# Local attention with a gated feed-forward layer on one core: the last scores of batch 0 placed ahead of its first value product, shifted values copied by GpSimd, and the first transposes of batch 1 moved to another PSUM pair

## The chip, the core and the metric

The kernel runs on one core of a Trainium2 chip. The metric is the device time of one execution in microseconds. In the text TensorE (PE in the profile, with its weight loads as PEld) does the matrix products and transposes, VectorE (DVE) and ScalarE (ACT) the elementwise work, GpSimd (POOL) and SP issue transfers; GpSimd also does a little elementwise work. L12 is line 12 of the kernel as the profile numbers it.

## The reference

Eight batches of eight heads attend over 576 tokens, with a window of 32 to either side and eight global tokens that see all and are seen by all. The result goes through a gated layer with 512 inputs and 1536 hidden columns.

```python
scores = scale * np.matmul(q, k.transpose(0, 1, 3, 2))
mask = np.abs(pos[:, None] - pos[None, :]) <= window
mask = mask | is_global[:, None] | is_global[None, :]
scores = np.where(mask, scores, -1000000000.0)
attn = softmax(scores)                       # over the keys
attn_out = np.matmul(attn, v)                # (8, 8, 576, 64)
x = attn_out.transpose(0, 2, 1, 3).reshape(4608, 512)
g = x @ w_gate
out = (g * sigmoid(g) * (x @ w_val)) @ w_out
```

## The kernel before

The attention of a batch is cut into steps, each a function that issues its instructions on all engines. In the order of the data they are:

- **step_T** (step_T0 for batch 0) transposes keys and queries of one pair of heads with TensorE (L355, L375) and copies them from PSUM into kT and qT. From batch 3 on a transposing DMA does this instead.
- **step_GT, step_SG, step_S2** handle the global tokens. GpSimd multiplies their gathered rows with a mask (kqm, L247), TensorE transposes them (L393), and products with all queries (SG) and all keys (S2) follow, each with an exponential and a mask product (pg at L416, p at L439).
- **step_P2T** transposes the masked S2 into p2t: by TensorE (L452) up to batch 3, by a transposing DMA from SP (L448) from batch 4 on. **step_AV2** multiplies p2t with the values (L462), and VectorE turns the sums into gvt (L469, L474, L477), which every value product of the batch reads.
- **step_S u**, u from 0 to 4, computes local scores: 64 queries against 128 keys a tile (L493), exponential on ScalarE (pe, L501), mask product on VectorE (pt, L507).
- **step_AV tp**, tp from 0 to 3, is the value product of 128 queries: a part from the global tokens (L546) and one from the window (L555), then the normalisation (den L522, L527 and xa L528). **step_AV8** does the last 64 queries.
- **step_X** transposes the result into xT, the input of the layer: by TensorE and a ScalarE copy (L604, L610) for batches 0 and 1, by a DMA later.

A value product takes its even 64-query tile from va, the values as loaded (128 tokens a block), and its odd one from **vb**, the same values shifted by 64 tokens. Since the shift crosses partitions, vb is made by a copy of each half of va into the other half of the partitions. Batch 0 makes it in vb0: VectorE copies the tiles 0 and 1 (L639, L640), two SP transfers the tiles 2 and 3 (L641, L642).

PSUM is held in three pools: "sc" (the score pair) and "m" with one pair of banks each, and "f" with four single banks. A step that allocates a buffer of a pool waits until the readers of the one that it replaces are done. Scores and some transposes lie in "sc", most of the other attention steps in "m", the layer's products in "f". For batch 0 several steps borrow "f", and the third gate of the first chunk (pgv) borrows "m".

The order of work is written out by hand, and each engine runs its instructions in the order in which they are issued. Batch 0 comes first, as one list of steps in which mask products and normalisations (the keys "p*", "xa*") are placed one by one, and warm(n), n products of constants into an unused "f" bank, stands between some of them. Behind it come the loads of batch 1 (loads_b, issued by GpSimd), and then the gates of the first 512 rows, column part by column part. From there on the layer's units (twelve gates, four outputs for each 512 rows) form a row of 144 slots, and the steps of batches 1 to 7 are dropped into the slots behind them. A batch b from 3 on has ten groups of steps that are spread over 16 slots from 16(b-1)+1 on.

A gate is eight products of 512 columns on TensorE (L711; L729 for the first two, done in parts), a tanh on ScalarE (th, L742) and two products on VectorE (gv, L744; h, L748); an output (L772) is twelve products and a ScalarE copy.

Of the kernel before, what the change touches and what calls it, by code (L numbers as in the profile page):

```python
# [26 lines left out]
def kernel(  # L27
# [11 lines left out]
    nc = tc.nc  # L39
# [32 lines left out]
    psc = ctx.enter_context(tc.tile_pool(name="psc", bufs=1, space=bass.MemoryType.PSUM))  # L72
    pm = ctx.enter_context(tc.tile_pool(name="pm", bufs=1, space=bass.MemoryType.PSUM))
# [50 lines left out]
    def load_vb(b):  # L124
        va = va_bufs[b % 2]
        vb = bp.tile([P, 4, H, W], BF16, tag="vb", name="vb")
        if b == 0:
            return vb
        nc.sync.dma_start(out=vb[0:64], in_=va[64:128, 0:4])
        nc.sync.dma_start(out=vb[64:128], in_=va[0:64, 1:5])  # L130
        return vb
# [39 lines left out]
    def clear(i):  # L171
# [10 lines left out]
        out=oh16.rearrange("p h a r -> p (h a r)"),  # L182
        in_=ident.rearrange("p (a g) -> p a g", g=NG), axis=AX.X, op=ALU.add,
# [3 lines left out]
        out=p8, in_=ident.rearrange("p (a g) -> p g a", g=NG), axis=AX.X, op=ALU.add  # L187
# [9 lines left out]
        out=tmp8h, in0=dmask.rearrange("p h r -> p (h r)"), in1=i8_f, op=ALU.mult  # L197
# [4 lines left out]
        out=gidx_f, in_=gidx_i64.bitcast(I32).rearrange("p (a b) -> p a b", b=2)[:, :, 0]  # L202
# [8 lines left out]
        out=hrow, in0=hrow, scalar1=float(S), scalar2=gcol, op0=ALU.mult, op1=ALU.add  # L211
# [4 lines left out]
        out=mka, in_=oh16.rearrange("p h a r -> p a r h"), axis=AX.X, op=ALU.add  # L216
# [6 lines left out]
        out=thr, in0=asel, scalar1=R2 + 0.25, scalar2=-0.25, op0=ALU.mult, op1=ALU.add  # L223
# [3 lines left out]
        out=sgn, in0=asel, scalar1=2.0, scalar2=-1.0, op0=ALU.mult, op1=ALU.add  # L227
# [3 lines left out]
        out=thi, in0=asel[:, 0:1], scalar1=1e6, scalar2=0.5, op0=ALU.mult, op1=ALU.add  # L231
# [13 lines left out]
    def gather_mask(kg, qg, kqm, eng=None):  # L245
        for a, src in ((0, kg), (1, qg)):
            (eng or nc.gpsimd).tensor_tensor(  # L247
                out=kqm[:, a], in0=bc(src, [[0, 2], [1, D]]),
                in1=bc(mka[:, a, :], [[1, 2], [0, D]]), op=ALU.mult,
            )  # L250
        return kqm
# [7 lines left out]
    def load_wgv(i):  # L259
# [13 lines left out]
        out=band, in_=band, compare_op=ALU.is_ge, fill=0.0,  # L273
# [3 lines left out]
        out=band, in_=band, compare_op=ALU.is_ge, fill=0.0,  # L277
# [60 lines left out]
    def attention(b):  # L338
        kT = kT_bufs[b % 2]
        va = va_bufs[b % 2]  # L340
        st = {}
# [21 lines left out]
        def step_T(hp):  # L363
            if hp == 0:
                qTs[b] = bp.tile([P, HP, S], BF16, tag="qT", name="qT")
            pool, tag = (pm, "m") if (hp in (0, 2) if b == 1 else hp == 3) else (psc, "sc")
            pair = pool.tile([P, 2, 1024], BF16, tag=tag, name="ps_t")
            pss = []
            for n, name in enumerate(("k", "q")):
                ps = pair[:, n, 0:S].rearrange("p (j i) -> p j i", j=LJ)  # L370
                pss.append(ps)
                src = loaded[b][name]
                for j in range(LJ):
                    for par in range(2):
                        nc.tensor.transpose(  # L375
                            out=ps[64 * par : 64 * par + 64, j, :],
                            in_=src[:, 2 * hp + par, D * j : D * (j + 1)],
                            identity=ident[0:LP, 0:LP],
                        )
            nc.scalar.copy(  # L380
                out=kT[:, hp, WIN : WIN + S].rearrange("p (i j) -> p i j", j=LJ),
                in_=pss[0].rearrange("p j i -> p i j"),
            )
            (nc.scalar.copy if hp % 2 else nc.vector.tensor_copy)(
                out=qTs[b][:, hp, :].rearrange("p (i j) -> p i j", j=LJ),
                in_=pss[1].rearrange("p j i -> p i j"),
            )
# [249 lines left out]
        def vb0(t):  # L637
            st["vb"] = load_vb(0)
            nc.vector.tensor_copy(out=st["vb"][0:64, 0:2], in_=va[64:128, 0:2])  # L639
            nc.vector.tensor_copy(out=st["vb"][64:128, 0:2], in_=va[0:64, 1:3])  # L640
            nc.sync.dma_start(out=st["vb"][0:64, 2:4], in_=va[64:128, 2:4])  # L641
            nc.sync.dma_start(out=st["vb"][64:128, 2:4], in_=va[0:64, 3:5])  # L642

        L = lambda f, *a: (lambda: f(*a))
        if b == 0:
            act, dve = nc.scalar.copy, nc.vector.tensor_copy

            M = lambda *key: (lambda: st[key if len(key) > 1 else key[0]]())
            def kqm0():
                kqms[0] = gather_mask(*g0, eng=nc.vector)  # L650

            return [
                L(squares), L(tables_a),
                L(step_T0, "k", 0, act), L(step_T0, "k", 1, act), L(tables_b), L(clear, 1),
                L(step_T0, "q", 0, act), L(step_T0, "q", 1, dve),
                L(step_T0, "k", 2, act), L(step_T0, "k", 3, act), kqm0, L(step_GT),
                L(step_S, 0), L(step_S2), M("p2*"), L(step_T0, "q", 2, dve),
                L(step_T0, "q", 3, act), L(step_P2T), L(step_SG), L(step_S, 1), M("p*", 0),
                L(vb0, 0), M("pg*"), L(step_AV2), M("p*", 1),
                L(step_S, 2), L(step_S, 3), L(warm, 2), L(step_AV, 0), M("p*", 2), M("xa*", 0),  # L660
                L(step_AV, 1), L(warm, 1), M("p*", 3), M("xa*", 1), L(step_X, 0),
                L(step_AV, 2), L(warm, 1), M("xa*", 2), L(step_X, 1), L(step_AV, 3), M("xa*", 3),
            ], [L(step_X, 2)], [L(step_X, 3)], [L(step_S, 4), M("p*", 4)], [L(step_AV8)], [L(step_X8)]
# [12 lines left out]
        if b < XQ:  # L676
            return [
                [L(step_T, 0)], [L(step_T, 1)],
                *([[L(step_T, 2)], [L(step_GT), L(step_T, 3), vb]] if b == 1 else
                  [[L(step_GT), L(step_T, 2)], [L(step_T, 3), vb]]),  # L680
            ] + mid + end
# [2 lines left out]
            [L(step_S2), L(step_SG)],  # L684
            [L(step_S, 0), L(step_P2T)],
            [],
            [L(step_S, 1)],
            [L(step_S, 2), L(step_AV2)],
            [L(step_S, 3), L(step_AV, 0), L(step_X, 0)],
            [L(step_AV, 1), L(step_X, 1)],  # L690
            [L(step_S, 4), L(step_AV, 2), L(step_X, 2)],
# [91 lines left out]


    head, xa2, xa3, s4, av8, x8 = attention(0)
    for f in head:
        f()
# [32 lines left out]
    for b, o in ((1, 2), (2, 15)):  # L820
        for i, g in enumerate(attention(b)):
            gaps[o + i] = gaps.get(o + i, []) + g
    for b in range(XQ, B):
        steps = attention(b)
        o = 16 * (b - 1)
        for i, g in enumerate(steps):
            slot = o + 1 + (16 * i) // len(steps)
            gaps[slot] = gaps.get(slot, []) + g
        if b > XQ:
            tr_at[b] = o - 16 + 5  # L830
        if b > 4:
            cast_at[b] = o - 32 + 8
        v_at[b] = o - 16 + 2
        g_at[b] = o - 16 + 6
        m_at[b] = o - 16 + 13
# [43 lines left out]
```

The softmax here doesn't subtract the row's maximum and nothing guards it: scores larger than these inputs give would overflow.

## Time and profile before

| | |
|---|---|
| median of six runs | 371.2 us (368.19 to 373.56) |
| the profiled execution | 370.38 us |
| its span | 368.7 us |
| mean granted clock of TensorE | 0.995 |
| busy: PE, DVE, ACT, POOL | 351.3, 235.4, 152.8, 97.5 us |
| matrix products of the layer's gates (L711) and outputs (L772) | 217.5 and 94.5 us |

The span runs from the first to the last instruction of one execution, and all times of the trace count from its start. The profiled execution's own time is 1.7 us longer than the span and 0.8 us under the median. A busy share is not the same as being the limit: the layer's products and the steps between them are what TensorE works through, and the other engines matter where TensorE waits for them. In the lines of the trace the first number is the start, the second the duration, both in us, and a bracket at the end gives how long the engine stood idle ahead of the row and what released it.

### The profile page before, as it was taken

How to read it: one execution, taken by the hardware profiler on the slowest of the kernel's cores; microseconds unless marked ns; L12 is line 12 of the kernel's file. 1: busy time of each engine (PE TensorE's matmuls, PEld its weight loads, DVE VectorE, ACT ScalarE, POOL GpSimd, SP SyncE). 2: the span in 40 equal slices, each digit the busy share in tenths (PEclk: the TensorE clock that was granted, in tenths of full speed). 3: DMA queues.
4: the chain of work that ended last, by engine and by line, in shares of the span. 5: the costliest groups of instructions: out<-in, count | busy, mean ns of one | idle time of the engine just before them, and what ended most of it. 6: DMA issues, size and time to landing. Idle time of an engine off the chain costs nothing.

```text
span 368.7 us, 7993 instructions
## 1 busy us (share of the span) xinstructions
PE 351.3 (95%) x3290; PEld 175.8 (48%) x3290; DVE 235.4 (64%) x469; ACT 152.8 (41%) x237; POOL 97.5 (26%) x114
## 2 busy tenths in 40 slices
PE   3786999999999999999999999999999999999996
PEld 2564545554544444444544445444544454444444
DVE  6665678268962885488548863887388728724750
ACT  5633574357422652255325523543344323313322
POOL 7924564953236001460137012200000000000000
PEclk9999899999999999999999999999999999999999
DMA  6999999999999946899979999961340131011002
GB/s 104 143 209 204 119 199 197 162 205 157 146 150 140 199 78 83 143 136 155 144 137 149 145 140 145 160 97 45 114 100 2 31 107 44 0 57 60 0 6 110
DMA packets 141637, 43.52 MB, mean 118 GB/s; under 512 B 126368, under 2 KB 135840, under 8 KB 141600
## 3 DMA queue, kind: packets, MB, share of 16 engines
q0 software_dynamic: 93824, 19.40, 61.6%
q1 hardware_dynamic: 47776, 23.60, 30.8%
q8 instruction: 26, 0.43, 0.5%
q14 instruction: 11, 0.09, 0.1%
HBM read 38.28 MB, written 15.34 MB: 145 GB/s over the span
## 4 chain that ended last, share of the span: by engine, by line
PE 88%; DVE 5%; DMA 3%; ACT 3%; issue 1%; POOL 0%; SPq 0%; POOLq 0%; DVEq 0%
PE pg L711 25%; PE po L772 25%; PE pv L711 23%; PE ps_av L546 3%; PE ps_s L493 3%; PE ps_av L555 2%; DMA vb<-va 2%; ACT pe L501 2%; PE ps_t L375 1%; DMA k_bf<-in_k_dram 1%; DVE pt L507 1%; DVE gvt L469 1%; PE ps_s L427 1%; PE po L759 1%; DVE h L748 1%
## 5 line engine op out<-in xcount | busy, mean ns | idle before, releaser
L711 PE MATMUL pg<-xT,wg_sb 128*128 128x512 bf16 x420 | 108.8, 381 | 0.0
L711 PE MATMUL pv<-xT,wv_sb 128*128 128x512 bf16 x420 | 108.7, 382 | 0.0
L744 DVE SCALAR_TENSOR_TENSOR gv<-th,pg 128x512 bf16<-128x512 bf16 x107 | 73.3, 685 | 41.8 <-ACT th L742 41.2
L742 ACT ACTIVATE th<-pg 128x512 bf16<-128x512 f32 x107 | 63.9, 598 | 80.9 <-PE pg L711 78.0
L772 PE MATMUL po<-wo_sb,h 128*128 128x512 bf16 x420 | 94.5, 379 | 0.0
L748 DVE TENSOR_TENSOR h<-gv,pv 128x512 bf16<-128x512 bf16 x107 | 73.6, 688 | 11.8 <-PE pg L711 0.5
L711 PEld LDWEIGHTS <-wv_sb 128*128 128x128 bf16 x424 | 41.7, 98 | 50.7 <-issue 1.1
L102 POOL DMA_DIRECT2D va<-in_v_dram x40 | 35.2, 963 | 103.5 <-PE ps_av L555 78.0
L772 PEld LDWEIGHTS <-h 128*128 128x128 bf16 x420 | 39.9, 98 | 46.4
L711 PEld LDWEIGHTS <-wg_sb 128*128 128x128 bf16 x424 | 37.1, 98 | 40.9 <-issue 1.7
L777 ACT ACTIVATE osb<-po 128x512 f32<-128x512 f32 x35 | 20.9, 597 | 81.7 <-PE po L772 77.7
L501 ACT ACTIVATE pe<-ps_s 128x1024 bf16<-128x1024 f32 (+1 forms) x40 | 37.5, 938 | 18.7 <-PE ps_s L493 18.0
L507 DVE TENSOR_TENSOR pt<-pe,band 128x1024 bf16<-128x1024 bf16 (+1 forms) x40 | 25.4, 636 | 20.3 <-ACT pe L501 20.3
L522 DVE TENSOR_REDUCE den<-ps_av 128x8 f32<-128x16 f32 (+1 forms) x40 | 6.7, 168 | 35.9 <-PE ps_av L555 33.6
L528 DVE TENSOR_TENSOR xa<-ps_av,den 128x512 bf16<-128x512 f32 (+1 forms) x40 | 25.5, 638 | 1.5 <-DMA xT<-xa 0.2
L546 PE MATMUL ps_av<-gvt,pg 128*64 128x264 bf16 x128 | 18.1, 296 | 0.9 <-DVE gvt L477 0.9
L493 PEld LDWEIGHTS <-kT 64*128 64x128 bf16 x576 | 11.3, 98 | 15.9 <-issue 15.0
L555 PE MATMUL ps_av<-vb,pt 128*64 128x66 bf16 x256 | 17.7, 198 | 0.5 <-DMA vb<-va 0.5
L555 PEld LDWEIGHTS <-pt 128*64 128x64 bf16 x512 | 17.6, 114 | 0.9 <-DMA vb<-va 0.7
L555 PE MATMUL ps_av<-va,pt 128*64 128x66 bf16 x256 | 17.8, 198 | 0.0
L493 PE MATMUL ps_s<-qT,kT 64*128 64x64 bf16 x576 | 16.2, 196 | 1.1 <-ACT pe L501 1.1
L109 POOL DMA_DIRECT2D qf<-in_q_dram x5 | 13.5, 2693 | 2.9 <-DMA va<-in_v_dram 2.9
(122 smaller groups left out, 223.2 us busy)
## 6 DMA issues: line engine op xcount, KB each, us to landing
out_dram<-osb SPq DMA_DIRECT2D x35, 256.0 KB, 2.1
vb<-va SPq DMA_DIRECT2D x14, 264.0 KB, 4.7
va<-in_v_dram POOLq DMA_DIRECT2D x24, 128.0 KB, 17.1
kf<-in_k_dram POOLq DMA_DIRECT2D x5, 576.0 KB, 10.2
qf<-in_q_dram POOLq DMA_DIRECT2D x5, 576.0 KB, 17.7
k_bf<-in_k_dram POOLq DMA_DIRECT2D x6, 288.0 KB
q_bf<-in_q_dram POOLq DMA_DIRECT2D x6, 288.0 KB, 4.2
va<-in_v_dram POOLq DMA_DIRECT2D x16, 96.0 KB, 8.2
```

The costliest lines, as they stand in the source:

```text
L102: nc.gpsimd.dma_start(out=va[lo:hi, u, :, 0:D], in_=vs[t0 + lo : t0 + hi])
L493: nc.tensor.matmul(out=ps[:, par, 64 * slot : 64 * slot + 64], lhsT=kT[r : r + 64, hp, 64 * t : 64 * t + P], rhs=qTs[b][r : r + 64, hp, 64 ...
L501: nc.scalar.activation(out=pe, in_=ps[:, :, 0 : 64 * ns].rearrange("p r (s c) -> p r s c", c=64), func=AF.Exp, scale=SCALE,)
L507: mult = lambda: nc.vector.tensor_tensor(out=pt.rearrange("p r s c -> p (r s) c"), in0=pe.rearrange("p r s c -> p (r s) c"), in1=bc(band, ...
L528: nc.vector.tensor_tensor(out=xa.rearrange("p (g h) d -> p g h d", g=g), in0=bc(ps, pst + [[1, D]]), in1=bc(den, [[4, g], [1, 4], [0, D]]) ...
L546: nc.tensor.matmul(out=ps[64 * e : 64 * e + 64, hg], lhsT=st["pg"][:, P * tp + 64 * e : P * tp + 64 * e + 64], rhs=st["gv"].rearrange("p h ...
L555: nc.tensor.matmul(out=ps[64 * e : 64 * e + 64, hg, hl, :], lhsT=pt[:, hl % 2, 4 * (hl // 2) + 2 * (tp % 2) + e, :], rhs=(va if e == 0 els ...
L711: nc.tensor.matmul(out=ps[:, 0:n], lhsT=w[:, cc, P * fc : P * (fc + 1)], rhs=xT[:, cc, t0 : t0 + n], start=(cc == 0), stop=(cc == NCC - 1),)
L742: nc.scalar.activation(out=th[:, 0:n], in_=pg[:, 0:n], func=AF.Tanh, scale=0.5)
L744: nc.vector.scalar_tensor_tensor(out=gv[:, 0:n], in0=th[:, 0:n], scalar=1.0, in1=pg[:, 0:n], op0=ALU.add, op1=ALU.mult,)
L748: nc.vector.tensor_tensor(out=st["h"][:, fc, 0:n], in0=gv[:, 0:n], in1=pv[:, 0:n], op=ALU.mult)
L772: nc.tensor.matmul(out=po, lhsT=st["h"][:, fc, P * ts : P * (ts + 1)], rhs=wo_sb[:, fc, :], start=(fc == 0), stop=(fc == NFC - 1),)
```

## The change

It has four places.

1. step_T 0 of batch 1 takes the pool "sc" in place of "m", and its copy of the transposed queries is made by ScalarE, which makes the copy of the keys too, in place of VectorE.
2. In vb0, the tiles 2 and 3 of vb are copied by two GpSimd instructions in place of two SP transfers.
3. In batch 0's list, warm(2) stands between step_S 2 and step_S 3; before, it stood behind both. step_S 3 is thus directly ahead of step_AV 0.
4. For batches 3 to 7, step_AV2 stands behind step_S 1, in the fifth group, and no longer behind step_S 2 in the sixth.

```diff
         def step_T(hp):
...
-            pool, tag = (pm, "m") if (hp in (0, 2) if b == 1 else hp == 3) else (psc, "sc")
+            pool, tag = (pm, "m") if hp == (2 if b == 1 else 3) else (psc, "sc")
...
-            (nc.scalar.copy if hp % 2 else nc.vector.tensor_copy)(
+            (nc.scalar.copy if hp % 2 or (b == 1 and hp == 0) else nc.vector.tensor_copy)(
                 out=qTs[b][:, hp, :].rearrange("p (i j) -> p i j", j=LJ),
                 in_=pss[1].rearrange("p j i -> p i j"),
             )
...
             nc.vector.tensor_copy(out=st["vb"][0:64, 0:2], in_=va[64:128, 0:2])
             nc.vector.tensor_copy(out=st["vb"][64:128, 0:2], in_=va[0:64, 1:3])
-            nc.sync.dma_start(out=st["vb"][0:64, 2:4], in_=va[64:128, 2:4])
-            nc.sync.dma_start(out=st["vb"][64:128, 2:4], in_=va[0:64, 3:5])
+            nc.gpsimd.tensor_copy(out=st["vb"][0:64, 2:4], in_=va[64:128, 2:4])
+            nc.gpsimd.tensor_copy(out=st["vb"][64:128, 2:4], in_=va[0:64, 3:5])
...
-                L(step_S, 2), L(step_S, 3), L(warm, 2), L(step_AV, 0), M("p*", 2), M("xa*", 0),
+                L(step_S, 2), L(warm, 2), L(step_S, 3), L(step_AV, 0), M("p*", 2), M("xa*", 0),
...
             [L(step_S, 0), L(step_P2T)],
             [],
-            [L(step_S, 1)],
-            [L(step_S, 2), L(step_AV2)],
+            [L(step_S, 1), L(step_AV2)],
+            [L(step_S, 2)],
             [L(step_S, 3), L(step_AV, 0), L(step_X, 0)],
```

## The prediction

> **What bounds the kernel.** I read first the page's slices and its chain, then the trace by stretches of time, then the waits of TensorE.
>
> ```profile
> PE   3786999999999999999999999999999999999996
> PEclk9999899999999999999999999999999999999999
> PE 88%; DVE 5%; DMA 3%; ACT 3%; issue 1%; POOL 0%; SPq 0%; POOLq 0%; DVEq 0%
> ```
>
> TensorE sets the end: from the fifth slice on (a slice is 9.2 us) it is busy all the time. Off that bound are only the first four, and the one low digit of the clock comes right behind them (slice five, 36.9 to 46.1 us). So a change pays if it closes a TensorE gap before 37 us or one of the small ones later; what it does on other engines costs only if TensorE comes to wait. The last of the early gaps by stretches of time, and what ended it:
>
> ```profile
> core 0: us, PE busy (x) PEld busy (x) DVE busy (x) ACT busy (x) POOL busy (x), PEclk, DMA share, GB/s
> 32.40:35.00 2.60, 0.08 (x3) 0.12 (x4) 2.37 (x5) 0.60 (x1) 1.58 (x2) 1.00 1.29 207
> 35.00:38.80 3.80, 3.80 (x34) 1.56 (x35) 1.45 (x2) 1.24 (x2) 0.21 (x1) 0.64 1.28 208
> ```
> ```profile
> 31.28 0.60 ACT L501 ACTIVATE pe<-ps_s 128x512 bf16<-128x512 f32 x1 [0.43 <-PE ps_s L493]
> 34.23 0.69 DVE L748 TENSOR_TENSOR h<-gv,pgv 128x512 bf16<-128x512 bf16 x1
> 34.97 0.45 PE L375 MATMUL ps_t<-ident,k_bf 96*64 96x96 bf16 x12 [2.52 <-DVE h L748]
> ```
>
> TensorE stands for 2.52 us before the first transposes of batch 1, since they write the "m" pair that the third gate (pgv) still holds; then it runs at a clock of 0.64.
>
> **Part 1: the first transposes go to the score pair.** They then wait for the last reader of "sc", the exponential of step_S 4 at 31.28, done at 31.88, and TensorE reaches them at 32.45. The 2.52 us go. Next in line is the data: GpSimd's value loads (L102) waited for q_bf until 32.87 and for the next k_bf until 34.33, so the first q_bf landed at about 32.8. That would leave some 0.3 us, but Part 2 takes load off the DMA, so I cost it at nothing.
> The low clock goes too. From 35.67 to 39.98 the chain shows fc 3, step_AV8 and the second transposes in 4.31 us; later rows have the same work at full clock as 0.97 + 0.86, 0.23 + 0.13 and 0.63 = 2.82. So 1.5 us more. Here the Trainium skill (TensorE: Matmul & The Clock Gate, "What's actually happening") speaks against me: it lets the clock fall after an idle window of about 3.4 us. By that rule a gap of 2.5 us loses no clock and this term is 0; by the row it is 1.5 us. The row is this gap itself, so I take 1.5.
> The other query copy moves from VectorE (0.76 us) to ScalarE (about 0.6), which delays fc 3's tanh by some 0.2 us; the four "f" banks hide this, and fc 4 would need its banks only 1 us later.
>
> **Part 2: shifted values by GpSimd, S 3 ahead of the first value product.** Gone are two SP transfers (L641, L642; 6.9 us to landing) and this wait:
>
> ```profile
> 20.49 0.13 PEld L546 LDWEIGHTS <-pg 128*64 128x64 bf16 x2 [0.83 <-DVE pt L507]
> 24.02 0.20 PEld L555 LDWEIGHTS <-pt 128*64 128x64 bf16 x7 [0.74 <-DMA vb<-va]
> ```
>
> S 3 starts at 18.98 either way (it waits for the exponential of S 2). The warm-up pair (1.03 us) moves from behind S 3 into the 1.12 us stall ahead of it, so the first value product could start at 19.66, when its mask product is done, in place of 20.49: up to 0.8 us. Against this stands the price of the copies. GpSimd has no such row; the nearest with one input are the two selects:
>
> ```profile
> 1.09 0.29 POOL masks.py:199 TENSOR_SCALAR_AFFINE_SELECT ident<-ident 128x128 bf16<-128x128 bf16 x1
> 13.08 0.24 POOL L272 TENSOR_SCALAR_AFFINE_SELECT band<-band 128x64 bf16<-128x64 bf16 x1
> 90.86 0.69 DVE L507 TENSOR_TENSOR pt<-pe,band 128x1024 bf16<-128x1024 bf16 x1
> 90.95 0.85 POOL L247 TENSOR_TENSOR kqm<-kg,mka 128x128 bf16<-128x128 f32 x1 [4.33 <-DMA kg<-in_k_dram,gofs]
> 91.77 0.39 POOL L247 TENSOR_TENSOR kqm<-qg,mka 128x128 bf16<-128x128 f32 x1
> ```
>
> Slope 0.83 ns an element, fixed 0.185 us: 1056 elements take 1.06 us. By the two-input product (0.39 us for 128) it would be 1.9 us. I take 1.06, the one-input row. Begun at about 17.0, both are done by 19.5 to 20.5; they are needed at 23.3, so even 1.9 us each hides.
> What does not hide is VectorE. At 90.95 the GpSimd product took 0.85 in place of 0.39, ending 0.34 us after VectorE's two-input mask product: one stood still for the other. The Trainium skill (SBUF — State Buffer, "Who interferes with whom") gives it as a lock, held for a whole instruction by whichever comes first, between a VectorE operation with two SBUF inputs and a GpSimd one that reads SBUF. The rows show only GpSimd waiting. By the rows alone VectorE loses nothing and the value product starts at 19.7; by the rule pg (L416), the small gvt (L477) and the mask product of S 1 (18.29 to 18.97) stand behind the copies: copy 17.0 to 18.1, pg to 18.5, copy to 19.6, then gvt and the mask product to 20.4. The start is 20.4, the gain gone. I take the rule. Of the vanished wait at 24.02 some 0.3 us survive, as the second output's normalisation (done 24.41) is what step_X 1 needs next: the first gates start 0.3 us earlier.
> Queued behind the copies on GpSimd are the loads of batch 1 (16.75 to 19.4), now about 3 us later. The transfers ahead of them land until 30 us, so the queue stays full: nothing. SP had nothing else to issue until 46 us.
>
> **What is late next.** Sum so far: 0.3 + 2.5 + 1.5 = 4.3 us at step_GT of batch 1, which TensorE finished at 44.5. But that step needs GpSimd's kqm:
>
> ```profile
> 41.10 0.40 POOL L247 TENSOR_TENSOR kqm<-kg,mka 128x128 bf16<-128x128 f32 x1 [5.89 <-DMA kg<-in_k_dram,gofs]
> ```
>
> kqm was done at 41.86, held by a gather behind the weights, and TensorE would now come at 40.05. The DMA is full at about 205 GB/s; without the 264 KB of Part 2 it runs ahead by 1.3 us at that rate, by 0.8 from the rates of 20 to 24 us. With 1.0 kqm is ready at 40.86, and 0.8 us of the gain are lost waiting. **Early part: -3.5 us** (between -2.2 and -4.3).
>
> **Part 3: step_AV2 of batches 3 to 7 one step earlier.** TensorE waits five times for its result:
>
> ```profile
> PE ps_av L546 <- DVE gvt L477: 0.9, 5, 0.2
> 197.73 1.70 SPq L448 DMA_TRANSPOSE p2t<-p x1
> DMA to landing us min/median/max: 9.3/9.3/9.3
> 205.77 0.41 PE L493 MATMUL ps_s<-qT,kT 64*128 64x64 bf16 x16
> ```
>
> The 0.9 us go. But from batch 4 on its input p2t comes by a transposing DMA. For batch 5 (these rows) it was issued at 197.73 and landed 9.3 us later, at 207.0; step_AV2 now follows S 1, done at 206.1. That is a new wait of 0.9 us where there was none (it stood at 210.0). Batch 4's landing isn't shown; issued at 160.24 under the same load, with a step at 168.55, it may wait nothing up to 3.9 us (it waited for nothing at 172.44). I take batch 5's 9.3: 1.0 us. Batches 6 and 7 landed in 2.7 and 3.4 us, no wait; batch 3 has no such DMA. The three VectorE instructions (1.05 us) now lie behind the mask product of S 1; banks for the gate after next are still free some 0.9 us ahead. **Part 3: -0.9 + 1.9 = +1.0 us** (between -0.9 and about +6.9).
>
> **The time.** -3.5 + 1.0 = -2.5 us against the profiled execution, 370.4 (span 368.7 and 1.7 around it): 367.9. The median of the six runs is 0.8 higher, 371.2, so I predict 368.7.
>
> **Rivals.**
> - Forecast, chance 0.45: 368.7, own range 367.3 to 370.
> - *The DMAs do better* (0.25). p2t of batches 4 and 5 lands in time: the early part (-3.5, or -4.3 if kqm is in time too) and -0.9 give 366.0 to 366.8. For it: the landing of one batch is all that is shown. Against it: that landing.
> - *GpSimd's copies hold the scores* (0.17). At 1.9 us each, with the lock, the mask product ends at about 22.4, the first value product 1.9 us late: which leaves 4.0 - 1.9 = 2.1 us of the early part and, with +1.0, 370.1 in all. For it: the two-input row; against it: the selects.
> - *p2t comes late* (0.13): the slower side. If batches 4 and 5 land as late as the old places allow at most, 172.4 and 210.0, TensorE waits 3.9 us each: -3.5 - 0.9 + 7.8 = +3.4, that is 374.6. It decides when both waits together pass 4.4 us, thus when p2t takes about 10.6 us from issue, against the 9.3 seen; batch 4's SP row (3.10 us against 1.70) speaks for it.
>
> **How the numbers follow.** The forecast, most of the two middle rivals and the mild half of the last lie between 365.8 and 372.5; about 2 in 10 is left out, with the half microsecond by which medians of such runs wander. About 1% (3.7 us) is what a measurement of this kernel can tell from no change. Faster by more: most of the second case and a little of the first, 0.29. Slower by more: the worse half of the last and a tail of the third, 0.13. Within: 0.58.
>
> **What would show it.** Right: the 2.52 us wait at L375 gone and a clock of 1.00 from 35 to 39 us; copies of about 1.1 us on POOL with a stretched L416 or L507 beside them; the value product at about 20.4; a new wait of L393 for kqm of under 1 us; no wait of L546 for gvt; L462 waiting on p2t in batches 4 and 5. Wrong: L375 waiting for q_bf, the low clock coming back, copies over 2 us, or L462 without a wait.

## The result, and the profile after

| | before | after |
|---|---|---|
| median | 370.61 us (71 runs) | 367.57 us (34 runs) |
| ratio | | 0.9928, 95% interval 0.9912 to 0.9944 |
| profiled execution, its span | 370.38, 368.7 us | 368.05, 366.3 us |

The kernel is 0.7% faster, 2.7 us by the ratio. To read the times below one has to know that the mean granted clock of an execution is either about 1.00 (full clock) or about 0.995 (low clock), for the kernel before as for the changed one, and that the medians of the two kinds lie 1.6 us or more apart; the part on the clock, further down, takes this up.

The slices and the chain on the page of the changed kernel:

```profile
PE   3899899999999999998999999999999999999996
PEclk9999999999999999999999999999999999999999
PE 78%; DMA 15%; POOL 4%; DVE 1%; issue 1%; ACT 1%; POOLq 0%; DVEq 0%
PE po L772 25%; PE pg L711 21%; PE pv L711 20%; DMA p2t<-p 5%; DMA kg<-in_k_dram,gofs 4%; DMA wg_sb<-in_moe_w_gate_dram 3%; PE ps_av L546 3%; DMA vb<-va 2%; PE ps_s L493 2%; PE ps_av L555 2%; POOL va L102 1%; DMA va<-in_v_dram 1%; PE po L759 1%; PE ps_av L462 1%; PE ps_t L375 1%
```

The low digit of TensorE's fourth slice and that of its clock are gone. An 8 has come in slice five (36.6 to 45.8 us) and one in slice nineteen (165 to 174 us), and the chain, nearly all TensorE before, now runs through transfers that it did not have: kg, the gather of batch 1, with the gate weights (wg_sb) ahead of it, and p2t. The two stretches of the old gap:

```profile
32.40:35.00 2.60, 2.60 (x44) 1.46 (x42) 2.46 (x5) 1.57 (x4) 1.15 (x2) 1.00 1.25 204
35.00:38.80 3.80, 3.80 (x41) 2.01 (x40) 3.09 (x7) 2.95 (x6) 0.00 (x0) 1.00 1.54 199
```

The columns are those shown before: TensorE is busy throughout (0.08 us of 2.60 before) at a clock of 1.00 (0.64 before). The row of pg before, and then the time line of the changed kernel around vb:

```profile
17.02 0.46 DVE L416 TENSOR_TENSOR pg<-pge,mg 128x576 bf16<-128x576 bf16 x1
```
```profile
16.98 1.06 POOL L641 COPY vb<-va 64x1056 bf16<-64x1056 bf16 x1 [0.20 <-DMA va<-in_v_dram]
17.04 1.31 DVE L416 TENSOR_TENSOR pg<-pge,mg 128x576 bf16<-128x576 bf16 x1
18.10 1.18 POOL L642 COPY vb<-va 64x1056 bf16<-64x1056 bf16 x1
19.23 1.28 DVE L507 TENSOR_TENSOR pt<-pe,band 128x1024 bf16<-128x1024 bf16 x2
19.83 0.43 PE L546 MATMUL ps_av<-gvt,pg 128*64 128x264 bf16 x2
```

The copies take 1.06 and 1.18 us. pg, 0.46 us before, is stretched to 1.31 and ends 0.31 us after the first copy: VectorE stood still for GpSimd. The first value product starts at 19.83 us (20.49 before). Then the transposes and the gathered rows, and step_AV2 of batches 4 and 5:

```profile
31.39 0.45 PE L375 MATMUL ps_t<-ident,k_bf 96*64 96x96 bf16 x12
40.05 0.40 POOL L247 TENSOR_TENSOR kqm<-kg,mka 128x128 bf16<-128x128 f32 x1 [5.93 <-DMA kg<-in_k_dram,gofs]
40.50 0.59 PE L393 MATMUL ps_g<-ident,kqm 128*128 128x128 bf16 x2 [1.29 <-DVE h L748]
...
166.09 0.47 PE L462 MATMUL ps_av<-va,p2t 128*32 128x132 bf16 x20 [1.19 <-DMA p2t<-p]
204.35 0.47 PE L462 MATMUL ps_av<-va,p2t 128*32 128x132 bf16 x20 [0.89 <-DMA p2t<-p]
```

The first transposes start with no wait, 3.6 us earlier than before. step_GT (L393) waits 1.29 us; the bracket names VectorE's h (L748), long done, but the row starts at 40.50, when the first kqm ends (40.05 + 0.40). The last transposes of batch 1 follow at 41.02 us, 3.4 us earlier than before. From there to the end 1 us is given back, at L462.

### The profile page after: what moved, and what is told of

It is laid out like the page before. It is cut to its first block, busy times and chain, and to the rows that moved or that the text cites. A ratio compares the mean times of both kernels' runs of the same rounds, so it can differ in the third digit from the quotient of the medians.

```text
span 366.3 us, 7991 instructions
## 1 busy us (share of the span) xinstructions
PE 349.8 (96%) x3290; PEld 175.0 (48%) x3290; DVE 236.0 (64%) x468; ACT 153.2 (42%) x238; POOL 99.1 (27%) x116
## 4 chain that ended last, share of the span: by engine, by line
PE 78%; DMA 15%; POOL 4%; DVE 1%; issue 1%; ACT 1%; POOLq 0%; DVEq 0%
PE po L772 25%; PE pg L711 21%; PE pv L711 20%; DMA p2t<-p 5%; DMA kg<-in_k_dram,gofs 4%; DMA wg_sb<-in_moe_w_gate_dram 3%; PE ps_av L546 3%; DMA vb<-va 2%; PE ps_s L493 2%; PE ps_av L555 2%; POOL va L102 1%; DMA va<-in_v_dram 1%; PE po L759 1%; PE ps_av L462 1%; PE ps_t L375 1%
## 5 line engine op out<-in xcount | busy, mean ns | idle before, releaser
L744 DVE SCALAR_TENSOR_TENSOR gv<-th,pg 128x512 bf16<-128x512 bf16 x107 | 73.3, 685 | 40.4 <-ACT th L742 39.8
L748 DVE TENSOR_TENSOR h<-gv,pv 128x512 bf16<-128x512 bf16 x107 | 73.6, 688 | 11.1
L711 PEld LDWEIGHTS <-wg_sb 128*128 128x128 bf16 x424 | 37.0, 98 | 40.9 <-issue 1.7
## 6 DMA issues: line engine op xcount, KB each, us to landing
va<-in_v_dram POOLq DMA_DIRECT2D x24, 128.0 KB, 17.9
```

The costliest lines, as they stand in the source:

```text
L711: nc.tensor.matmul(out=ps[:, 0:n], lhsT=w[:, cc, P * fc : P * (fc + 1)], rhs=xT[:, cc, t0 : t0 + n], start=(cc == 0), stop=(cc == NCC - 1),)
L744: nc.vector.scalar_tensor_tensor(out=gv[:, 0:n], in0=th[:, 0:n], scalar=1.0, in1=pg[:, 0:n], op0=ALU.add, op1=ALU.mult,)
L748: nc.vector.tensor_tensor(out=st["h"][:, fc, 0:n], in0=gv[:, 0:n], in1=pv[:, 0:n], op=ALU.mult)
```

## The experiments

Each run's time is the median on its chip, beside the kernel before on the same chip; the ratio has its 95% interval. A run with a larger share of low clock than the kernel before has a higher median for that alone, so where the shares differ the two kinds are compared each with its own.

**The parts alone, one chip, kernel before at 369.74 us.** First, the transposes of batch 1 alone:

```diff
-            pool, tag = (pm, "m") if (hp in (0, 2) if b == 1 else hp == 3) else (psc, "sc")
+            pool, tag = (pm, "m") if hp == (2 if b == 1 else 3) else (psc, "sc")
...
-            (nc.scalar.copy if hp % 2 else nc.vector.tensor_copy)(
+            (nc.scalar.copy if hp % 2 or (b == 1 and hp == 0) else nc.vector.tensor_copy)(
```

> The kernel before with the first place of the change alone (first transposes of batch 1 in the score pair, both copies by ScalarE). My theory: the 2.5 us wait at L375 and the low clock behind it go, but without the relief of the DMA the gathered rows come no earlier than before (kqm at about 41.9 us), so that step_GT of batch 1 takes back what is over about 2.5 us: -2.5 us at the transposes behind it and at the end, a wait of TensorE at L393 of about 1.3 us or more. Rival, that the transposes only trade one wait for another (on q_bf): a wait of over 1 us at L375 and less than 1.5 us gained.

Measured: 367.77 us, ratio 0.9949 (0.9925 to 0.9973), -1.9 us by the ratio. Its time line:

```profile
32.60 0.45 PE L375 MATMUL ps_t<-ident,k_bf 96*64 96x96 bf16 x12
40.97 0.40 POOL L247 TENSOR_TENSOR kqm<-kg,mka 128x128 bf16<-128x128 f32 x1 [5.94 <-DVE gv L744]
41.43 0.59 PE L393 MATMUL ps_g<-ident,kqm 128*128 128x128 bf16 x2 [1.01 <-POOL kqm L247]
```

No wait at L375, so the rival falls; kqm holds L393, for 1.01 us where 1.3 or more were expected, and the next transposes come at 41.94, 2.5 us earlier than before. At full clock the medians are 367.50 us (11 executions) and 369.24 before (15), 1.7 us apart.

The second and third place alone (vb by GpSimd, the warm products ahead of step_S 3):

```diff
-            nc.sync.dma_start(out=st["vb"][0:64, 2:4], in_=va[64:128, 2:4])
-            nc.sync.dma_start(out=st["vb"][64:128, 2:4], in_=va[0:64, 3:5])
+            nc.gpsimd.tensor_copy(out=st["vb"][0:64, 2:4], in_=va[64:128, 2:4])
+            nc.gpsimd.tensor_copy(out=st["vb"][64:128, 2:4], in_=va[0:64, 3:5])
...
-                L(step_S, 2), L(step_S, 3), L(warm, 2), L(step_AV, 0), M("p*", 2), M("xa*", 0),
+                L(step_S, 2), L(warm, 2), L(step_S, 3), L(step_AV, 0), M("p*", 2), M("xa*", 0),
```

> The kernel before with the second and third place alone (vb by GpSimd, warm products ahead of step_S 3). My theory: the first gates start about 0.9 us earlier, as in the changed kernel, the wait at the first transposes stays at 2.5 us and the low clock behind it too, so about -0.9 us in all, and kqm about 1 us earlier without use. Rival, that the copies on GpSimd cost through the lock on VectorE what the transfers cost: 0 us at the first gates and at the end.

Measured: 370.19 us, ratio 1.0012 (0.9992 to 1.0032): by the ratio nothing is gained, against 0.9 us expected. But 10 of its 12 executions had the low clock, and 11 of 26 before. Each kind with its own, it is 0.5 us shorter (370.35 against 370.85 us at the low clock, 368.70 against 369.24 at the full one, where it has two executions only). In its trace the first gates start at 25.46 us, 0.34 earlier than before and not 0.9, as the value product waited 0.63 us for gvt; the wait at L375 is 2.52 us. The first kqm was ready at 39.8 us while L393 came at 43.69: the room that these places make on the DMA is of no use as long as the transposes stand still.

The fourth place alone, and the changed kernel without it:

```diff
-            [L(step_S, 1)],
-            [L(step_S, 2), L(step_AV2)],
+            [L(step_S, 1), L(step_AV2)],
+            [L(step_S, 2)],
```

> The kernel before with the fourth place alone (step_AV2 of batches 3 to 7 behind step_S 1). My theory: five waits of 0.19 us go, two waits on p2t of about 1 us come (batches 4 and 5): +1.1 us. Rival, that the waits on p2t only move idle time that TensorE would have had later: 0 or -0.9 us.

> The changed kernel without its fourth place (step_AV2 back behind step_S 2). My theory: the two waits on p2t go, five of 0.19 us come back, 1.1 us faster than the changed kernel, thus about -3.5 us against the kernel before. Rival, as above: no faster than the changed kernel, -2.5 us.

Measured: 371.55 us, ratio 1.0045 (1.0019 to 1.0070), +1.7 us alone; and 365.98 us, ratio 0.9907 (0.9877 to 0.9936), -3.4 us without it. Neither settles the price. The first run had the low clock in 7 of 9 executions: at the low clock it took 371.56 us against 370.85 before, at the full clock 368.83 against 369.24 (two executions), and in its trace, of a full-clock execution, the two waits on p2t are 0.7 us together, less than the 0.9 us of waits on gvt that went. The interval of the second run still holds the rival's -2.5 us; in its trace TensorE has the five waits on gvt again (1.0 us in all) and none on p2t. The comparison was made once more beside the changed kernel itself, on a third chip (before: 369.69 us):

> The changed kernel once more, as the yardstick for the three others on the same chip: about 2.7 us under the kernel before, with a granted clock of 0.995 in about one execution of five, and two waits on p2t of 0.4 to 1.6 us in the trace.

> The changed kernel without its fourth place, beside the changed kernel. My theory: 1.0 us faster than it (the waits on p2t less five of 0.19 us). Rival, that the waits on p2t hide time due anyway: the same time.

Measured: 367.37 us (0.9960, 0.9927 to 0.9994) and 366.17 us (0.9904, 0.9874 to 0.9933): in this kernel the fourth place costs 1.2 us, and 1.1 at full clock (367.23 us in 10 executions against 366.17 in 11), so the rival falls. The late waits of TensorE (total, count, longest, in us) in the kernel before with the fourth place alone, in the changed kernel on this chip, and in the changed kernel without its fourth place:

```profile
PE ps_av L462 <- DMA p2t<-p: 0.7, 2, 0.6
PE ps_av L462 <- DMA p2t<-p: 2.6, 2, 1.3
PE ps_av L546 <- DVE gvt L477: 1.0, 5, 0.2
```

The same edit thus brought waits of 0.7 us in one kernel and of 2.1 and 2.6 us in the other: what it costs hangs on when p2t lands (that of batch 5, 8.6 us after its issue in the first of the two, 9.3 and 9.7 us in the traces of the second).

**What TensorE waits for late, a second chip, kernel before at 369.22 us.** step_AV2 early only where p2t is there in time:

```diff
-            [L(step_S, 1), L(step_AV2)],
-            [L(step_S, 2)],
+            [L(step_S, 1)] + ([] if b in (4, 5) else [L(step_AV2)]),
+            [L(step_S, 2)] + ([L(step_AV2)] if b in (4, 5) else []),
```

> The changed kernel, with step_AV2 early for batches 3, 6 and 7 alone. My theory: no wait on p2t, and the 0.19 us waits stay in batches 4 and 5 alone: 2.1 - 0.4 = 1.7 us faster than the changed kernel, about -4.3 us against the kernel before. Rival, that the waits on p2t hide time due anyway: as the changed kernel, -2.5 us.

Measured: 365.12 us, ratio 0.9904 (0.9873 to 0.9935), -3.5 us by the ratio and -4.1 by the medians. No wait on p2t, two of 0.2 us on gvt. The trace is the theory's. The time lies between the two forecasts, and the interval still holds the rival's -2.5 us; what speaks against that rival is the comparison on the third chip above.

The tiles 2 and 3 of vb by SP again, in the changed kernel:

> The changed kernel with the tiles 2 and 3 of vb by the two SP transfers again. My theory: TensorE waits for vb before the third value product as before, pg (L416) falls back from 1.31 to 0.46 us, the DMA queue is later by about 1 us, and so are kqm and all behind it: some 0.8 to 1.0 us slower than the changed kernel, about -1.6 us against the kernel before. Rival, that the copies hardly matter since kqm bounds the stretch anyway: -2.5 us.

Measured: 367.72 us, ratio 0.9970 (0.9942 to 0.9997), -1.1 us. pg took 0.46 us again, TensorE waited 1.2 us for vb, and kqm came at 40.61 (40.05 and 39.31 in the two traces of the changed kernel). The trace is as the theory has it, but the time settles nothing: the interval touches that of the changed kernel's first measurement (0.9912 to 0.9944) and covers its ratio on the third chip (0.9960). What the copies by GpSimd are worth in the changed kernel is not shown.

The gathers ahead of the weights:

```diff
         load_qk_part(1, loaded[1], 1)
-        load_wgv(2)
         g1 = gather(1)
+        load_wgv(2)
         load_v(1, range(0, 3))
```

> The changed kernel with the gathers of batch 1 issued ahead of the third pair of gate weights. My theory: kqm is no longer behind 1 MB of weights, the wait of TensorE at L393 (1.3 us, and what follows it up to the next transposes, 1.5 us in all) goes, 1.3 to 1.5 us faster than the changed kernel, about -4.1 us against the kernel before. Rival, that the next data (values of batch 1, weights of the ninth gate) are late then and take it back: -2.5 us.

Measured: 365.36 us, ratio 0.9902 (0.9870 to 0.9934), -3.6 us. Its time line:

```profile
32.65 0.45 PE L375 MATMUL ps_t<-ident,q_bf 96*64 96x96 bf16 x12 [1.06 <-DMA q_bf<-in_q_dram]
35.83 0.40 POOL L247 TENSOR_TENSOR kqm<-kg,mka 128x128 bf16<-128x128 f32 x1 [0.66 <-DMA kg<-in_k_dram,gofs]
```

Both kqm are ready 3.5 us ahead of their use, and L393 (40.05) waits no more. In this execution the queries came late instead and took 1.06 us of it; in the last run below, with the same order of loads, they did not. The changed kernel was not run on this chip, so how much of the -3.6 us is due to the gathers is open here.

**The clock.** The kernel before, with products of constants in the gap:

```diff
+    at(2, warm, 8)
     for b, o in ((1, 2), (2, 15)):
```

> The kernel before with eight products of constants (warm) put into the wait ahead of the first transposes of batch 1. The transposes start when they did. By my theory the low clock behind them comes from the 2.5 us in which TensorE stood still: the clock stays at 1.00 from 35 to 39 us and the kernel is 1.3 to 1.5 us faster. By the rule [...] the wait was not the cause: clock and time as before.

Measured: 368.11 us, ratio 0.9984 (0.9961 to 1.0006), 1.1 us less by the medians; the ratio alone does not tell it from no change. What tells is the clock of each execution. In the profiled one the values of batch 0 came late, so that the first transposes started at 36.25 us, and 0.79 us of the gap were left. Here are the two stretches in this run, and then in the run with the fourth place alone, which still has the gap:

```profile
32.40:35.00 2.60, 2.60 (x13) 1.18 (x12) 2.43 (x5) 0.82 (x2) 1.38 (x2) 1.00 1.29 208
35.00:38.80 3.80, 3.01 (x37) 1.46 (x36) 2.13 (x4) 1.24 (x2) 0.42 (x1) 1.00 1.24 208
```
```profile
32.40:35.00 2.60, 0.17 (x9) 0.17 (x10) 2.31 (x4) 0.54 (x1) 1.71 (x2) 1.00 1.28 207
35.00:38.80 3.80, 3.64 (x68) 2.21 (x65) 2.25 (x5) 1.75 (x3) 0.00 (x0) 1.00 1.28 208
```

The second pair has the same gap as the kernel before, a wait of 2.52 us at L375, and no low clock behind it. The trace of the second and third place alone has that wait too, and a clock of 0.64 from 35.0 to 38.8 us. So the gap does not bring the low clock every time. By the mean clock of the single executions:

| chip | before, clock 1.00 | before, clock under 0.998 | executions with the low clock |
|---|---|---|---|
| first | 369.24 us | 370.85 us | 11 of 26 |
| second | 367.88 us | 369.57 us | 13 of 23 |
| third | 367.79 us | 369.92 us | 19 of 28 |
| second, gap filled | 368.05 us | 370.91 us | 1 of 12 |

With the gap filled the kernel takes what the kernel before takes at full clock, and the low clock comes once in twelve; with the gap closed, in the run of the first place alone, it comes once in twelve too. So my theory holds for the gap as a cause, but as a chance of 43 in 77; what decides in an execution was not seen. The changed kernel had it in 8 of 36 executions, and in 2 of 12 on the third chip, where it then took 370.28 us against 367.23. Where its low clock lies is open: no trace of such an execution was taken. The kernels here without the gap and with step_AV2 early in all five batches had it in 14 of 78 executions, those without the gap and with step_AV2 late at least in batches 4 and 5 in 2 of 41. That points to the waits on p2t, but it mixes chips and kernels and shows no cause.

**GpSimd or VectorE for the copies, third chip.**

```diff
-            nc.gpsimd.tensor_copy(out=st["vb"][0:64, 2:4], in_=va[64:128, 2:4])
-            nc.gpsimd.tensor_copy(out=st["vb"][64:128, 2:4], in_=va[0:64, 3:5])
+            nc.vector.tensor_copy(out=st["vb"][0:64, 2:4], in_=va[64:128, 2:4])
+            nc.vector.tensor_copy(out=st["vb"][64:128, 2:4], in_=va[0:64, 3:5])
```

> The changed kernel with all four copies of vb made by VectorE. My theory: a GpSimd copy holds pg (L416) from 17.0 to 18.0 us through the lock; two more VectorE copies of 0.43 and 0.50 us put pg at the same place, 17.9 to 18.4, so that the value product and the end stay where they are, within 0.3 us of the changed kernel. Rival, that GpSimd's copies are work taken off VectorE: 0.9 us slower than the changed kernel.

Measured: 366.63 us, ratio 0.9930 (0.9902 to 0.9958), against 367.37 us of the changed kernel beside it. The rival falls: that GpSimd makes two of the copies saves no time here. pg came at 18.34 (my 17.9 was too early, as the two copies took 0.67 and 0.65 us) and the value product at 19.77, where it was. The 0.7 us by which it is ahead were not expected, and the two intervals overlap; its profiled execution had shorter waits on p2t (1.03 and 0.51 us).

**Both mends together**, step_AV2 early for batches 3, 6 and 7 alone and the gathers ahead of the weights:

> The changed kernel with step_AV2 early for batches 3, 6 and 7 alone and the gathers of batch 1 ahead of the third pair of gate weights. My theory: both gains add, 1.7 us without the waits on p2t and about 1 us for kqm less the wait on q_bf that the gathers cause, 2.5 to 3 us faster than the changed kernel. Rival, that one of them covers the other: 1.7 us.

Measured: 363.88 us, ratio 0.9848 (0.9803 to 0.9892), 3.5 us under the changed kernel on the same chip and the shortest time of all runs. The gains add, and the 1.7 us of the rival are passed: the interval lies under that of the changed kernel (0.9927 to 0.9994). TensorE waits neither on p2t nor on the kqm of batch 1, and the first query transposes start at 31.68 us without a wait:

```profile
34.61 0.40 POOL L247 TENSOR_TENSOR kqm<-kg,mka 128x128 bf16<-128x128 f32 x1 [0.66 <-DVE gv L744]
39.05 0.28 PE L393 MATMUL ps_g<-ident,kqm 128*128 128x128 bf16 x2
```

## Why the prediction was right

It said 368.7 us, 2.5 us less; measured are 2.7 by the ratio, from a slightly lower level. The mechanism came as forecast in the main, with the exceptions told below. That the whole sum fits the medians too has some luck in it: it takes in the low clock as certain, and on the three chips just over half of the executions before had it, so that their median lies near the low kind, while the changed kernel's lies with the full clock.

- **First transposes.** The 2.52 us went, with no wait for q_bf. Right.
- **The low clock**, the step that was mis-sized. As the price of one occurrence 1.5 us was near (1.6 to 2.1 us between the two kinds of executions before), and the profiled execution had it. But it was put into the sum as certain, and it comes in 43 of 77 executions. So the sum fitted the pair of profiled executions (370.38 and 368.05 us, 2.3 less) and not the others. For an execution before at full clock the prediction's own steps give less: step_GT ended at 44.5 - 1.5 = 43.0 there, kqm lets TensorE go on at 40.9, so about -2 early, +1.0 late, -1 us in all. On the third chip the changed kernel at clock 1.00 took 367.23 us against 367.79 before, -0.6 us (10 and 9 executions, too few to tell it from -1 or from 0); the rest of the 2.3 us between that chip's medians is that the low clock became rarer (2 of 12 against 19 of 28).
- **Rule against row for the clock.** The row was taken against the rule that the prediction gives from the Trainium skill (TensorE: Matmul & The Clock Gate, "What's actually happening"), an idle window of about 3.4 us. Neither was enough: a gap of 2.5 us can bring the low clock, and with the gap filled it is nearly gone, so the rule alone would have missed it; but the same gap also passed without it, so the row alone counted it too often. One profiled execution cannot show a chance.
- **The copies and the lock.** 1.06 us was right to the digit for the first, 1.18 for the second. VectorE was held as the rule said that the prediction gives from the Trainium skill (SBUF — State Buffer, "Who interferes with whom"): pg took 1.31 us in place of 0.46. (By the two rows at 90.86 and 90.95 us that the prediction shows, the GpSimd product ended 0.25 us after the mask product, not 0.34; nothing rests on it.) The order was not the one forecast: pg waited for the first copy alone, gvt and the mask product for hardly anything, and the value product started at 19.83 and not at 20.4. So the first gates gained 0.9 us (24.88 against 25.80) and not 0.3. In the run of the second and third place alone the start was 20.31 and the gain 0.34: the forecast's case comes too.
- **kqm late.** It was done at 40.80 us, 1.06 earlier than before (1.0 forecast), and TensorE waited. The 0.6 us that the earlier first gates brought beyond the forecast were lost here: the early part was -3.4 us against -3.5. That is one execution: in the second trace of the changed kernel kqm started at 39.31, the wait was 0.57 us and the last transposes came at 40.28 (41.02 in the first). That it was this wait is shown by the two runs with the gathers ahead of the weights, where kqm is early, L393 does not wait, and the last transposes come at 40.26 and 39.26.
- **p2t.** Waits of 1.19 and 0.89 us, 1.0 and 0.9 forecast; the five of 0.19 us went. The part cost 1.2 us on the third chip, 1.1 at full clock (1.0 forecast). Batch 4's landing, unknown then, was 9.6 us.

Of the rivals, *copies hold the scores* had its mechanism but not its price, *p2t comes late* did not come (landings of 8.2 to 10.0 us in all traces that show one for batches 4 and 5, under the 10.6 that decide), and *the DMAs do better* is, for p2t, what the run with step_AV2 early in batches 3, 6 and 7 alone builds.

## What to carry to other kernels

A gap that is closed lets the engine run into the next late input: work out when that one arrives before the gap is counted as gained, since two changes that each bring little (a wait removed, room made on the DMA) can be worth more together than alone (here, at full clock on one chip, 1.7 and 0.5 us alone and 3.3 together, on few executions). Moving a step nearer to the producer of its input is only safe for those iterations where the input has landed; look the landing up for each of them, not for the typical one. And read the clock of single executions: a cost that comes in half of them belongs into a sum with its share, and two kernels are compared kind with kind.

## What the runs showed of the hardware

A copy by GpSimd can hold an operation of VectorE, and which of the two comes first differs from trace to trace of kernels that are alike up to there. In the last run pg came first, and a later product of eight columns was held:

```profile
16.93 0.46 DVE L416 TENSOR_TENSOR pg<-pge,mg 128x576 bf16<-128x576 bf16 x1
16.94 1.37 POOL L641 COPY vb<-va 64x1056 bf16<-64x1056 bf16 x1 [0.30 <-DMA va<-in_v_dram]
18.37 1.06 POOL L642 COPY vb<-va 64x1056 bf16<-64x1056 bf16 x1
18.51 0.97 DVE L477 TENSOR_TENSOR gvt<-lo,gvt 128x8 bf16<-128x8 f32 x1
```

L477 takes 0.20 us alone; here 0.97, to the end of the second copy. In the second trace of the changed kernel without its fourth place it was a VectorE copy, with one input, that stood behind GpSimd's:

```profile
16.69 1.13 POOL L641 COPY vb<-va 64x1056 bf16<-64x1056 bf16 x1
16.93 1.18 DVE L640 COPY vb<-va 64x1056 bf16<-64x1056 bf16 x1
18.14 1.20 DVE L416 TENSOR_TENSOR pg<-pge,mg 128x576 bf16<-128x576 bf16 x1
```

L640 takes 0.50 us in the kernel before, and at most 0.71 in the traces where it ends before GpSimd's copies begin or where GpSimd makes none. The value product behind all this started between 19.5 and 20.3 us in the kernels with GpSimd's copies.
